# Widening a seven-product matrix product by two blocks, and moving its neighbour's partial sums into all eight PSUM banks

## The chip, the cores and the metric

One core of one Trainium2 chip runs the whole kernel. The metric is device time in microseconds (us). Three timed runs of the kernel before the change gave 512.77, 513.73 and 514.19 us; the median is 513.73 us.

## The reference

Two blocks stand one after the other. The first is a delta-rule attention over 4 batches, 8 heads, 768 positions and head size 48. The second is a three-way maxout feed-forward layer on the 3072 x 384 result.

```python
for t in range(S):                                   # attention, per batch and head
    y[t] = q[t] @ state
    v_old = k_n[t] @ state
    state += beta[t] * outer(k_n[t], v[t] - v_old)
x = y.transpose(0, 2, 1, 3).reshape(3072, 384)
h = max(max(x @ w1, x @ w2), x @ w3)                 # 384 -> 768, three times
out = h @ w_out                                      # 768 -> 384
```

All arithmetic is in 32-bit floats.

## The kernel before

**Tiling.** The sequence is cut into 12 chunks of 64 positions. Two chunks of all four batches make a group of 512 tokens, so there are six groups, m = 0 to 5. The attention of a group is done as small matrix products per head (lines with `p_g`, `p_z`, `p_j`, `p_k`, `p_q`, `p_u`, `p_s`, `p_y`) and a triangular solve on VectorE (L552, L556). The feed-forward layer of group m (`ffn(m)`) is the steady work of TensorE; the attention steps of group m+1 are laid between its pieces by hand.

**The order of the work.** The schedule is manual: each engine runs its instructions in the order in which the Python code emits them. `ffn(m)` is a generator; after each `yield` number i the main loop (L1427 to L1444) emits the attention steps that the table `LINKS` (or `LAST_LINKS` for m = 4) names for i. In that table `K0` to `K3` load four key tiles of the next group through GpSimd's queue (`load_k`, L120), and `P0`, emitted before or after them, scales a value tile on GpSimd (L287). The table names K at i = 17, so the loads of keys 4(m+2) to 4(m+2)+3 are issued while `ffn(m)` runs its output products; for m = 3 these are keys 20 to 23. Key n lies in tile `kpad[n % 4]` from n = 12 on.

**The algebra of the feed-forward layer.** From group 1 on the kernel uses max(a, b, c) = a + max(0, b - a, c - a): `less_first` replaces W2 and W3 by W2-W1 and W3-W1, and `both_layers` puts the product W1·Wo (384 x 384) into `w_sb[0][:, t, 0:384]`. The output is then h'·Wo + x·(W1Wo).

**Groups 4 and 5, the output.** `outputs(m, hs)` (L947) computes h'·Wo + x·(W1Wo) for a group. The first term goes by a seven-product scheme: the tokens are halved, the 768 hidden features are halved into two times `PAIRS` = 3 blocks of 128, and the 384 output columns are halved. Seven products replace eight; the sums of left operands (`s32`, `s14`) are made on VectorE, and the sums of right operands (t1 to t4) once in `cross_weights`. Each product is 3 blocks x 2 token tiles = 6 matmuls with 128 x 128 stationary and 128 x 192 moving operands. The second term is added plainly by four `x_times`, each 3 blocks x 2 = 6 matmuls. That makes 66 matmuls per group. Two PSUM tiles `p` and `q` take turns; ScalarE copies products out, VectorE adds.

**Group 5, the first layer.** `crossed_hidden` (L1067) does x·(W2-W1) and x·(W3-W1) by the same scheme on two of the three blocks of x; the third block is added plainly (`c1`, `c2`). It loops over six units. A unit has eight partial results, and each is one or two matmuls of 128 x 256, 11 in all. Partial results 0, 2, 3 and 4 are copied out by ScalarE (m1, m7, m5, m6); 1, 5, 6 and 7 are added by VectorE (`result`, L1108), which also does four additions between 4 and 5 and, in every second unit, four maxima (L1110). `s1` to `s4`, the sums of x's parts, are made once per group in `kmore[0]`.

**PSUM.** There are two pools of tiles, defined at L80 to L84: `ps_ffn` hands out 2 tiles of one bank each, `ps_two` hands out 3 tiles of two banks each, 8 banks together. In `crossed_hidden`, `bank(n)` takes a `ps_ffn` tile for odd n (named `p_e`) and a fresh `ps_two` tile for even n (`p_c`), of which it uses the first bank alone.

A matmul of 32-bit floats shows in the trace as two MATMUL records and two weight loads, so "x12" in a row is 6 matmuls.

Of the kernel before, what the change touches and what calls it, by code (L numbers as in the profile page):

```python
# [14 lines left out]
ALU = mybir.AluOpType  # L15
# [8 lines left out]
def kernel(  # L24
# [37 lines left out]
    KT = DM // 128  # L62
# [3 lines left out]
    GROUPS = UNITS // 4  # L66
    TOK = 512
# [12 lines left out]
    def ps_ffn(shape, name):  # L80
        return psum.tile(shape, FP32, name=name, tag="ffn", bufs=2)

    def ps_two(name):
        return psum.tile([128, 2, 512], FP32, name=name, tag="two", bufs=3)  # L84


    kpad = [const.tile([128, H, DP], FP32, name=f"kpad{i}") for i in range(4)]
# [93 lines left out]
    for bb in range(2):  # L181
        nc.gpsimd.affine_select(
            out=mask[rows(bb)], in_=mask[rows(bb)], pattern=[[1, C]], base=-1,
# [4 lines left out]
    t1 = [const.tile([128, 2, H, BL], FP32, name=f"t1{i}") for i in range(NU)]  # L188
# [5 lines left out]
    w_sb = [const.tile([128, KT, DFF], FP32, name=f"w{i}_sb") for i in range(3)]  # L194
# [112 lines left out]
    def square(name):  # L307
        return work.tile([128, H, C], FP32, name=name, tag="square", bufs=17)
# [594 lines left out]
    HALF = DM // 2  # L903
    PAIRS = FT // 2
    crossed = {}

    def cross_weights(part):

        left, right = slice(0, HALF), slice(HALF, DM)
        top, bottom = wo_sb[:, 0:PAIRS], wo_sb[:, PAIRS:FT]  # L910
        spare = w_sb[0][:, :, DM : 2 * DM]
        minus = nc.vector.tensor_tensor
        if part == 0:
            minus(
                out=spare[:, :, right], in0=bottom[:, :, right], in1=top[:, :, right],
                op=ALU.subtract,
            )
            minus(
                out=top[:, :, right], in0=top[:, :, right], in1=top[:, :, left],
                op=ALU.subtract,  # L920
            )
            return
        minus(
            out=spare[:, :, left], in0=bottom[:, :, right], in1=top[:, :, right],
            op=ALU.subtract,
        )
        fourth = []
        for n in range(2):
            t = work.tile([128, DM], FP32, name="mant", bufs=2)
            for i in range(2 - n):  # L930
                fourth.append(t[:, HALF * i : HALF * (i + 1)])
        for j in range(PAIRS):
            minus(
                out=fourth[j], in0=wo_sb[:, PAIRS + j, left], in1=spare[:, j, left],
                op=ALU.subtract,
            )
        crossed.update(
            b11=[top[:, j, left] for j in range(PAIRS)],
            b21=[bottom[:, j, left] for j in range(PAIRS)],
            b22=[bottom[:, j, right] for j in range(PAIRS)],  # L940
            t1=[top[:, j, right] for j in range(PAIRS)],
            t2=[spare[:, j, left] for j in range(PAIRS)],
            t3=[spare[:, j, right] for j in range(PAIRS)],
            t4=fourth,
        )

    def outputs(m, hs):  # L947


        xt, w = xts[m], crossed  # L950
        a11, a21, a12, a22 = (
            [hs[j + d][:, lo : lo + 256] for j in range(PAIRS)]
            for d, lo in ((0, 0), (0, 256), (PAIRS, 0), (PAIRS, 256))
        )
        p, q = (ps_ffn([128, 2, HALF], "p_o") for _ in range(2))

        def times(to, a, b, start=True, stop=True):
            for g in range(2):
                for j in range(PAIRS):
                    nc.tensor.matmul(  # L960
                        to[:, g], a[j][:, 128 * g : 128 * (g + 1)], b[j],
                        start=(start and g == j == 0),
                        stop=(stop and g == 1 and j == PAIRS - 1),
                    )

        def x_times(to, lo, right, start=False, stop=True):
            times(
                to,
                [xt[:, t, lo : lo + 256] for t in range(KT)],
                [w_sb[0][:, t, HALF * right : HALF * (right + 1)] for t in range(KT)],  # L970
                start, stop,
            )

        def held(name, dtype_bufs):
            return work.tile([128, 2, HALF], FP32, name=name, bufs=dtype_bufs)

        def store(o, cc, right, queues=one_queue):
            cols = slice(HALF * right, HALF * (right + 1))
            s0 = (2 * m + cc) * C
            for n in range(2):  # L980
                queues[n].dma_start(
                    out=out.rearrange("(b s) d -> b s d", s=S)[
                        2 * n : 2 * n + 2, s0 : s0 + C, cols
                    ].rearrange("g c x -> c g x"),
                    in_=o[rows(n)],
                )

        def op(to, a, b, how):
            nc.vector.tensor_tensor(out=to, in0=a, in1=b, op=how)

        plus, minus = ALU.add, ALU.subtract
        times(p, a11, w["b11"])
        m1 = held("m1", 1)
        nc.scalar.copy(m1, p)
        yield
        sums = [square("s").rearrange("p h c -> p (h c)") for _ in range(PAIRS)]
        s14, s32 = ([s[:, lo : lo + 256] for s in sums] for lo in (0, 256))
        for j in range(PAIRS):
            op(s32[j], a11[j], a21[j], minus)
        for j in range(PAIRS):  # L1000
            op(s14[j], a21[j], a22[j], plus)
        times(q, a12, w["b21"], True, False)
        yield
        x_times(q, 0, 0)
        c11 = held("o_sb", 2)
        op(c11, m1, q, plus)
        store(c11, 0, 0)
        yield
        times(p, s32, w["t3"])
        m7 = held("o_sb", 2)  # L1010
        nc.scalar.copy(m7, p)
        yield
        times(q, s14, w["t1"])
        m5 = held("up", 2)
        nc.scalar.copy(m5, q)
        for j in range(PAIRS):
            op(s32[j], s14[j], a11[j], minus)
        yield
        times(p, s32, w["t2"])
        m6 = held("up", 2)  # L1020
        nc.scalar.copy(m6, p)
        for j in range(PAIRS):
            op(s14[j], a12[j], s32[j], minus)
        yield
        x_times(q, 0, 1, True, False)
        op(m6, m6, m1, plus)
        op(m7, m7, m6, plus)
        yield
        times(p, a22, w["t4"], True, False)
        op(m6, m6, m5, plus)  # L1030
        op(m5, m5, m7, plus)
        yield
        x_times(p, 256, 0)
        op(m7, m7, p, plus)
        store(m7, 1, 0)
        yield
        times(q, s14, w["b22"], False)
        op(m6, m6, q, plus)
        store(m6, 0, 1)
        yield  # L1040
        x_times(p, 256, 1, True)
        op(m5, m5, p, plus)
        store(m5, 1, 1, both_queues)
        yield

    thirds = {}

    def cross_hidden(i):

# [17 lines left out]
    def crossed_hidden(m, hs):  # L1067


        xt, vec = xts[m], nc.vector.tensor_tensor  # L1070
        plus = vec if m == GROUPS - 1 else nc.gpsimd.tensor_tensor
        lo, hi = slice(0, 256), slice(256, 512)
        a11, a12, a13 = (xt[:, t, lo] for t in range(KT))
        a21, a22, a23 = (xt[:, t, hi] for t in range(KT))
        spare = [t.rearrange("p a h d -> p (a h d)") for t in kmore]
        s1, s2, s3, s4 = (spare[0][:, 256 * n : 256 * (n + 1)] for n in range(4))
# [7 lines left out]
        vec(out=s1, in0=a21, in1=a22, op=ALU.add)  # L1084
        vec(out=s2, in0=s1, in1=a11, op=ALU.subtract)
        vec(out=s4, in0=a12, in1=s2, op=ALU.subtract)
        for j in range(FT):
            hs[j] = square("h").rearrange("p h c -> p (h c)")
        for unit in range(2 * PAIRS):
            j, i = divmod(unit, 2)  # L1090
            w = {
                name: t[:, 128 * j : 128 * (j + 1)]
                for name, t in thirds[1 + i].items()
            }
# [17 lines left out]
                    )  # L1112

            def bank(n):
                return (ps_ffn([128, TOK], "p_e") if n % 2 else ps_two("p_c")[:, 0])[
                    :, 0:256
                ]

            p = bank(0)
            times(p, ("b11", a11))  # L1120
            nc.scalar.copy(m1, p)
            p = bank(1)
            times(p, ("b21", a12), ("c1", a13))
            result(top[:, lo], m1, p, c11)
            p = bank(2)
# [222 lines left out]
    def links(m, names):  # L1348
        for name in names.split():
            f, i = name[0], int(name[1])  # L1350
            if f in RECURS and m < GROUPS:
                RECURS[f](2 * m + i)
            elif f in MADE and m + 1 < GROUPS:
                MADE[f](2 * (m + 1) + i)
            elif f in UNIT and m + 1 < GROUPS:
                UNIT[f](4 * (m + 1) + i)
            elif f == "N" and m + 2 < GROUPS:
                load_blocks(4 * (m + 2) + i)
# [115 lines left out]
```

## Time and profile before

| quantity | value |
|---|---|
| timed runs, median (lowest to highest) | 513.73 us (512.77 to 514.19) |
| profiled execution, first to last instruction | 510.5 us |
| TensorE busy with matmuls | 491.1 us, 96% of the span |
| VectorE, ScalarE, GpSimd busy | 349.9, 168.7, 192.7 us |
| first-layer units of group 5 (454.1 to 484.6 us): TensorE, VectorE, ScalarE busy | 29.6, 22.8, 8.9 of 30.0 us |
| output of group 5 (484.6 us to the end): TensorE, VectorE busy | 21.7, 10.6 of 25.9 us |
| mean granted TensorE clock | 0.966 |

The profiled execution's own device time is not given apart from its span; the median of the timed runs lies 3.2 us above the span, which is work around the first and the last instruction that the profile does not show.

TensorE has work nearly all the time, but matmul records overlap and their ends are modelled, so a full busy digit can still hold short waits. The waits are read from the gaps between the starts of consecutive matmuls in the timeline.

### The profile page before, as it was taken

How to read it: one execution, taken by the hardware profiler on the slowest of the kernel's cores; microseconds unless marked ns; L12 is line 12 of the kernel's file. 1: busy time of each engine (PE TensorE's matmuls, PEld its weight loads, DVE VectorE, ACT ScalarE, POOL GpSimd, SP SyncE). 2: the span in 40 equal slices, each digit the busy share in tenths (PEclk: the TensorE clock that was granted, in tenths of full speed). 3: DMA queues.
4: the chain of work that ended last, by engine and by line, in shares of the span. 5: the costliest groups of instructions: out<-in, count | busy, mean ns of one | idle time of the engine just before them, and what ended most of it. 6: DMA issues, size and time to landing. Idle time of an engine off the chain costs nothing.

```text
span 510.5 us, 18528 instructions
## 1 busy us (share of the span) xinstructions
PE 491.1 (96%) x8016; PEld 333.1 (65%) x8016; DVE 349.9 (69%) x801; ACT 168.7 (33%) x320; POOL 192.7 (38%) x317
## 2 busy tenths in 40 slices
PE   7778989999999999999999999999999999999996
PEld 6567778756565565665555565555655556998796
DVE  5897799969996430899563987635897455456752
ACT  5585664884422242210252101252101412113210
POOL 7434372783491926670575770503130000000000
PEclk9755999999999999999999999999999999999999
DMA  8938869764055925353675454923343202230001
GB/s 111 192 64 221 194 151 155 195 199 100 5 148 140 175 46 130 99 143 83 144 136 130 120 137 94 174 37 92 80 116 81 44 3 64 54 71 2 0 17 46
DMA packets 106304, 53.49 MB, mean 105 GB/s; under 512 B 89712, under 2 KB 99984, under 8 KB 106224
## 3 DMA queue, kind: packets, MB, share of 16 engines
q1 hardware_dynamic: 94352, 31.35, 30.4%
q0 software_dynamic: 9472, 20.37, 16.4%
q8 instruction: 63, 1.03, 0.9%
q10 hardware_dynamic: 2400, 0.59, 0.6%
q14 instruction: 17, 0.14, 0.1%
HBM read 39.17 MB, written 13.11 MB: 102 GB/s over the span
## 4 chain that ended last, share of the span: by engine, by line
PE 73%; DVE 14%; DMA 5%; ACT 4%; SPq 2%; issue 2%; POOL 0%; DVEq 0%; ACTq 0%; POOLq 0%
PE p_h L1161 26%; PE p_o L1199 13%; PE p_o L960 9%; PE p_e L1102 3%; DVE tmp L552 3%; PE p_g L406 3%; PE p_c L1102 2%; PE p_m L894 2%; PE p_u L759 2%; DMA kmore<-in_k_dram 2%; PE p_k L731 2%; PE p_y L801 2%; DVE y_bl L556 2%; PE p_s L782 2%; PE p_j L714 1%
## 5 line engine op out<-in xcount | busy, mean ns | idle before, releaser
L1161 PE MATMUL p_h<-xt,w_sb 128*128 128x512 f32 (+1 forms) x450 | 187.5, 558 | 0.7 <-ACT xt L827 0.6
L1161 PEld LDWEIGHTS p_h<-xt,w_sb 128*128 128x128 f32 x450 | 82.3, 193 | 68.7 <-issue 61.8
L1199 PE MATMUL p_o<-wo_sb,h 128*128 128x384 f32 x192 | 65.3, 490 | 0.0
L1175 DVE TENSOR_TENSOR h<-h,p_h 128x512 f32<-128x512 f32 (+1 forms) x42 | 25.4, 606 | 53.9 <-PE p_h L1161 52.8
L552 DVE TENSOR_TENSOR tmp<-x_bl,y_bl 128x31 f32<-128x31 f32 (+20 forms) x139 | 51.3, 369 | 4.1
L556 DVE TENSOR_TENSOR y_bl<-y_bl,tmp 128x31 f32<-128x31 f32 (+20 forms) x139 | 48.5, 349 | 4.8
L1199 PEld LDWEIGHTS p_o<-wo_sb,h 128*128 128x128 f32 x192 | 35.7, 190 | 23.2
L364 POOL DMA_DIRECT2D turned<-in_q_dram x72 | 39.1, 551 | 4.3 <-POOL turned L359 2.9
L1205 ACT COPY o_sb<-p_o 128x384 f32<-128x384 f32 x16 | 7.7, 479 | 85.8 <-PE p_o L1199 79.8
L1171 ACT ACTIVATE h<-p_h 128x512 f32<-128x512 f32 x24 | 14.3, 597 | 63.4 <-PE p_h L1161 60.5
L254 POOL TENSOR_TENSOR w_sb<-mant,up 128x384 int32<-128x384 int32 x18 | 19.1, 1059 | 39.3 <-DVE mant L250 39.2
L406 PEld LDWEIGHTS p_g<-kqt 48*64 48x64 f32 x1216 | 24.6, 142 | 9.0 <-issue 6.4
L406 PE MATMUL p_g<-kqt 48*64 48x64 f32 (+1 forms) x1216 | 27.8, 242 | 0.9 <-ACT kqt L335 0.8
L789 DVE TENSOR_TENSOR st<-st,p_s 48x768 f32<-48x768 f32 (+1 forms) x18 | 17.1, 949 | 15.4 <-PE p_s L782 15.2
L120 POOL DMA_DIRECT2D kpad<-in_k_dram x32 | 21.8, 690 | 14.1 <-issue 12.7
L1199 PE MATMUL p_o<-w_sb,xt 128*128 128x384 f32 x72 | 25.2, 486 | 0.0
L139 POOL DMA_DIRECT2D v_t<-in_v_dram x14 | 11.5, 829 | 35.5 <-PE p_u L759 35.5
L390 DVE TENSOR_TENSOR pt<-p_g,mask 128x512 f32<-128x512 f32 x20 | 13.8, 688 | 15.9 <-PE p_g L406 15.8
L287 POOL TENSOR_TENSOR v_t<-v_t,nrm 128x768 f32<-128x768 f32 x12 | 17.9, 1493 | 9.0 <-DVE nrm L281 8.9
L359 POOL MEMSET turned<- 128x96 f32 x18 | 3.3, 192 | 47.6 <-DVE kqt L380 47.6
L759 PEld LDWEIGHTS p_u<-v_t,ut 64*64 64x64 f32 x768 | 13.4, 141 | 10.1 <-issue 7.8
L1199 PEld LDWEIGHTS p_o<-w_sb,xt 128*128 128x128 f32 x72 | 13.7, 190 | 9.5
(212 smaller groups left out, 837.0 us busy)
## 6 DMA issues: line engine op xcount, KB each, us to landing
out_dram<-o_sb SPq DMA_DIRECT2D x40, 96.0 KB
w_bits<-in_moe_w_dram SPq DMA_DIRECT2D x9, 384.0 KB
w_bits<-in_moe_w_dram POOLq DMA_DIRECT2D x9, 384.0 KB, 5.2
turned<-in_q_dram POOLq DMA_DIRECT2D x72, 48.0 KB, 2.9
kpad<-in_k_dram POOLq DMA_DIRECT2D x32, 96.0 KB, 6.1
y_x<-y SPq DMA_DIRECT2D x16, 192.0 KB
qall<-y_x SPq DMA_DIRECT2D x32, 96.0 KB
v_t<-in_v_dram POOLq DMA_DIRECT2D x14, 192.0 KB, 5.0
```

The lines of the kernel that those rows point to most:

```text
L120: queues[bb].dma_start(out=dst[rows(bb ^ g), :, 0:D], in_=src[2 * bb + g, :, c * C : (c + 1) * C, :].rearrange("h p d -> p h d"),)
L254: nc.gpsimd.tensor_tensor(out=dst.bitcast(I32), in0=mant_v.bitcast(I32), in1=up_v, op=ALU.add)
L364: (queue, nc.gpsimd)[i].dma_start(out=t[p0 : p0 + 32, bb, at : at + NP * 2 * D].rearrange("p (j x) -> p j x", j=NP), in_=(k, q)[i][2 * bb ...
L406: nc.tensor.matmul(p_g[rows(bb ^ (g * i)), par, c0 : c0 + C * (1 + whole)], kq[:, 0], kq if whole else kq[:, i],)
L552: nc.vector.tensor_tensor(out=t_v, in0=row.to_broadcast(t_v.shape), in1=column.to_broadcast(t_v.shape), op=ALU.mult,)
L556: nc.vector.tensor_tensor(out=rest, in0=rest, in1=t_v, op=ALU.subtract)
L759: nc.tensor.matmul(p_v[rows(bb ^ g), g, i], ut[c % NU][rows(bb), g, h], rhs[rows(bb), g, h],)
L960: nc.tensor.matmul(to[:, g], a[j][:, 128 * g : 128 * (g + 1)], b[j], start=(start and g == j == 0), stop=(stop and g == 1 and j == PAIRS - 1),
L1102: nc.tensor.matmul(to, w[stays], moves, start=(n == 0), stop=(n == len(terms) - 1))
L1161: nc.tensor.matmul(p_h, w_sb[i][:, t, f * 128 : (f + 1) * 128], xt[:, t, lo : lo + w], start=(t == 0), stop=(t == KT - 1),)
L1175: nc.vector.tensor_tensor(out=h, in0=h, in1=p_h, op=ALU.max)
L1199: nc.tensor.matmul(p_o, stays, moves, start=(n == 0), stop=(n == len(terms) - 1))
```

## The change

Three edits.

1. **Output of groups 4 and 5.** Blocks 0 and 1 of x·(W1Wo) become a fourth pair of blocks in the seven products: each product now has 4 blocks x 2 = 8 matmuls, and `x_times` keeps only block 2, 2 matmuls. The sums of left operands get a fourth part: for group 4 it is made beside the others on VectorE (four more 128 x 256 operations); for group 5 `s1` to `s4` of `crossed_hidden` are used again through `x_sums`. The sums of right operands are four more VectorE operations of 128 x 192 in `cross_weights(1)`, put into the tiles `kpad[2]` and `kpad[3]`.
2. **PSUM in `crossed_hidden`.** Partial results 0 to 5 now use both banks of three `ps_two` tiles: 0 and 1 share a tile, 2 and 3, and 4 and 5. Partial results 6 and 7 use the two `ps_ffn` tiles.
3. **Keys.** Keys 22 and 23 are not loaded: only the state update of the last chunk would read them, and it is left out in both kernels (`step` returns at c = 11).

```diff
@@ cross_weights(1)
+        x11, x12, x21, x22 = (w_sb[0][:, t, lr] for t in range(2) for lr in (left, right))
+        free = [kpad[i].rearrange("p h d -> p (h d)") for i in (2, 3)]
+        x1, x2, x3, x4 = (f[:, lr] for f in free for lr in (left, right))
+        for to, a, b in ((x3, x22, x12), (x1, x12, x11), (x2, x22, x1), (x4, x21, x2)):
+            minus(out=to, in0=a, in1=b, op=ALU.subtract)
...
+        for name, x in dict(
+            b11=x11, b21=x21, b22=x22, t1=x1, t2=x2, t3=x3, t4=x4
+        ).items():
+            crossed[name].append(x)
@@ outputs
+        for a, t, lo in ((a11, 0, 0), (a21, 0, 256), (a12, 1, 0), (a22, 1, 256)):
+            a.append(xt[:, t, lo : lo + 256])
...
-                for j in range(PAIRS):
+                for j in range(len(a)):
...
-                [xt[:, t, lo : lo + 256] for t in range(KT)],
-                [w_sb[0][:, t, HALF * right : HALF * (right + 1)] for t in range(KT)],
+                [xt[:, KT - 1, lo : lo + 256]],
+                [w_sb[0][:, KT - 1, HALF * right : HALF * (right + 1)]],
...
-        sums = [square("s").rearrange("p h c -> p (h c)") for _ in range(PAIRS)]
+        n = len(x_sums.get(m, ())) == 0
+        sums = [square("s").rearrange("p h c -> p (h c)") for _ in range(PAIRS + n)]
         s14, s32 = ([s[:, lo : lo + 256] for s in sums] for lo in (0, 256))
+        s1, s2, s3, s4 = s14, s32, s32, s14
+        if not n:
+            s1, s2, s3, s4 = (s + [x] for s, x in zip((s1, s2, s3, s4), x_sums[m]))
...
-        times(p, s32, w["t3"])
+        times(p, s3, w["t3"])
@@ crossed_hidden
+        x_sums[m] = s1, s2, s3, s4
+        pair = [None]
...
             def bank(n):
-                return (ps_ffn([128, TOK], "p_e") if n % 2 else ps_two("p_c")[:, 0])[
-                    :, 0:256
-                ]
+                if n > 5:
+                    return ps_ffn([128, TOK], "p_e")[:, 0:256]
+                if n % 2 == 0:
+                    pair[0] = ps_two("p_c")
+                return pair[0][:, n % 2, 0:256]
@@ links
+            if f == "K" and 4 * (m + 1) + i > 4 * GROUPS - 3:
+                continue
```

More of the change, by code (lines that the diff above doesn't have):

```diff
@@ L962, in times @@
                         start=(start and g == j == 0),
-                        stop=(stop and g == 1 and j == PAIRS - 1),
+                        stop=(stop and g == 1 and j == len(a) - 1),
                     )
@@ L995, in outputs @@
         yield
-        sums = [square("s").rearrange("p h c -> p (h c)") for _ in range(PAIRS)]
+        n = len(x_sums.get(m, ())) == 0
+        sums = [square("s").rearrange("p h c -> p (h c)") for _ in range(PAIRS + n)]
         s14, s32 = ([s[:, lo : lo + 256] for s in sums] for lo in (0, 256))
[L998 to L1001, printed above, removed]
+        s1, s2, s3, s4 = s14, s32, s32, s14
+        if not n:
+            s1, s2, s3, s4 = (s + [x] for s, x in zip((s1, s2, s3, s4), x_sums[m]))
+        for j in range(len(sums)):
+            op(s3[j], a11[j], a21[j], minus)
+        for j in range(len(sums)):
+            op(s1[j], a21[j], a22[j], plus)
         times(q, a12, w["b21"], True, False)
@@ L1012, in outputs @@
         yield
-        times(q, s14, w["t1"])
+        times(q, s1, w["t1"])
         m5 = held("up", 2)
         nc.scalar.copy(m5, q)
-        for j in range(PAIRS):
-            op(s32[j], s14[j], a11[j], minus)
+        for j in range(len(sums)):
+            op(s2[j], s1[j], a11[j], minus)
         yield
-        times(p, s32, w["t2"])
+        times(p, s2, w["t2"])
         m6 = held("up", 2)
         nc.scalar.copy(m6, p)
-        for j in range(PAIRS):
-            op(s14[j], a12[j], s32[j], minus)
+        for j in range(len(sums)):
+            op(s4[j], a12[j], s2[j], minus)
         yield
@@ L1036, in outputs @@
         yield
-        times(q, s14, w["b22"], False)
+        times(q, s4, w["b22"], False)
         op(m6, m6, q, plus)
@@ L1044, in outputs @@
         yield
-    thirds = {}
+    thirds, x_sums = {}, {}
     def cross_hidden(i):
```

## The prediction

> **What bounds the kernel now.** I read the page first, for the engine that is always busy, and its clock.
>
> ```profile
> span 510.5 us, 18528 instructions
> PE 491.1 (96%) x8016; PEld 333.1 (65%) x8016; DVE 349.9 (69%) x801; ACT 168.7 (33%) x320; POOL 192.7 (38%) x317
> PEclk9755999999999999999999999999999999999999
> PE 73%; DVE 14%; DMA 5%; ACT 4%; SPq 2%; issue 2%; POOL 0%; DVEq 0%; ACTq 0%; POOLq 0%
> ```
>
> TensorE bounds the kernel, at full clock from about 55 us on, so a matmul taken out of the tail or a wait put into it moves the end one for one. Second I read the timeline of the first-layer units of group 5 (start, duration, engine, line; "x2" is one matmul). Part of one unit, its partial results 2 to 5:
>
> ```profile
> 481.07 0.59 PE L1102 MATMUL p_e<-kmore,crossed 128*128 128x256 f32 x2
> 481.27 0.37 ACT L1127 COPY y_bl<-p_c 128x256 f32<-128x256 f32 x1 [1.11 <-PE p_c L1102]
> 481.50 0.59 PE L1102 MATMUL p_c<-kmore,crossed 128*128 128x256 f32 x2
> 481.70 0.37 ACT L1130 COPY y_bl<-p_e 128x256 f32<-128x256 f32 x1
> 481.94 0.59 PE L1102 MATMUL p_e<-xt,w_sb 128*128 128x256 f32 x2
> 482.14 0.37 ACT L1134 COPY y_bl<-p_c 128x256 f32<-128x256 f32 x1
> ```
>
> Matmuls start every 0.43 us, and a ScalarE copy of one result runs while TensorE writes the next one into another tile (481.70 beside 481.50). That overlap is what edit 2 touches. A copy starts 0.63 us after the start of the matmul it reads (481.07 to 481.70) and takes 0.37 us. Third, what a wait costs, from the seam between two units and from the seam to the output:
>
> ```profile
> 474.44 0.42 DVE L1110 SCALAR_TENSOR_TENSOR h<-h,y_bl 128x256 f32<-128x256 f32 x1
> 474.46 0.73 PEld L1102 LDWEIGHTS p_e<-xt,w_sb 128*128 128x128 f32 x4 [0.32 <-DVE y_bl L1108]
> 484.14 0.41 DVE L1108 TENSOR_TENSOR y_bl<-y_bl,p_e 128x256 f32<-128x256 f32 x1
> 484.60 3.87 PEld L960 LDWEIGHTS p_o<-wo_sb,h 128*128 128x128 f32 x24 [0.75 <-DVE y_bl L1108]
> ```
>
> TensorE restarts 0.05 us after the releasing instruction's end (484.14 + 0.41 to 484.60), and the wait holds the weight load too. The rows of the two tiles (count, then shortest, median and longest in ns) give the rest: after a wait a matmul record is 483 ns, otherwise 379, so 0.10 us is lost on weights that were not loaded ahead.
>
> ```profile
> L1102 PE MATMUL p_e<-kmore,crossed x12: 379/379/483, 455.8 to 481.3; 128*128 128x256 f32 x12
> L1102 PE MATMUL p_c<-kmore,crossed x24: 379/379/379, 455.4 to 481.7; 128*128 128x256 f32 x24
> ```
>
> Fourth, GpSimd and VectorE around the key loads:
>
> ```profile
> 371.70 2.71 POOL L120 DMA_DIRECT2D kpad<-in_k_dram  x4 [12.66 <-issue]
> 373.39 2.80 DVE L552 TENSOR_TENSOR tmp<-x_bl,y_bl 128x252 f32<-128x252 f32 x1
> 374.42 1.49 POOL L287 TENSOR_TENSOR v_t<-v_t,nrm 128x768 f32<-128x768 f32 x1
> ```
>
> An addition of 0.42 us took 2.80 beside GpSimd's scaling.
>
> **Edit 2, the banks.** Six units take 454.06 to 484.70 (the restart plus 0.10), 30.6 us, against 66 matmuls x 0.4325 = 28.5, so 2.1 us of waits are all that freer banks could give back. Partial results 0 and 1 now share a tile, as do 2 and 3, and 4 and 5. In the changed kernel's instruction stream the first matmul of results 1, 3 and 5 waits for the ScalarE copy of result 0, 2 and 4 *of the same unit*: the order is kept by tile, not by bank. In the old stream these matmuls waited for readers in earlier units. Price of one such wait: from the start of the even result's matmul to the end of its copy 0.63 + 0.37, restart 0.06, weights 0.10, less the 0.43 that it takes anyway: 0.73 us. Below, 0.57, if the weights get loaded ahead and the restart is free; above, 0.83, if the copy starts 0.73 after its matmul, as it does after a matmul that had waited (476.04 to 476.77). I take 0.73, the same copy on the same shapes behind an unhindered matmul. Three waits in six units: 18 x 0.73 = 13.1.
>
> A unit is then 4.76 + 2.19 = 6.95 us. VectorE needs at most 12 operations, four at 0.40 and four pairs at 0.79, 4.8 us a unit, so it stays under TensorE and the old 0.32 waits are gone. Six units are 41.7. Two seams come on top. In the first unit the copy of result 0 stands behind a store that ScalarE issues (454.84 for 0.68, the copy at 455.56, 1.50 after the matmul instead of 0.63): +0.87, now waited for; at least 0 if the store is out earlier. At the end the output's tile `p` takes over the buffer of result 6 instead of 5: counted from the last unit's start, copy m6 ends at 4.61, four additions to 6.26, the pair of result 5 to 7.05, the addition of result 6 at 7.46, restart 7.62 where 6.95 was free: +0.7 (before: 0.6). Sum 43.3 against 30.6: **+12.7**.
>
> On this point the Trainium skill, "PSUM — Partial Sum Buffer", section "PSUM bank collisions raise a hardware error", asks for a guard per bank and partition quadrant, and lets different banks be used at once. The rows above agree with it, a copy from one bank beside writes to another. By that rule alone the wait is not needed by the chip and edit 2 would cost nothing; the built stream has it all the same, and the stream is what runs.
>
> **Edit 1, the output.** 7 x 8 + 4 x 2 = 64 matmuls instead of 66. The 132 records of group 5 take 21.73 us on the chain, 0.33 a matmul: -0.65 a group. One cover shrinks: between the product for m6 and the next use of `p` stood an `x_times` of 6 matmuls, now of 2 (0.65 us), while the copy ends 0.68 after that `x_times` starts (496.41 to 497.09) and the restart adds 0.16: +0.2. So -0.45 for each of two groups, **-0.9**; between 0 and -1.3. VectorE's additions: 4 x 0.35 in group 4's sums lie before 434 us, needed after the p_y products at 437; the four weight sums, 4 x 0.35 = 1.4, fall into the 1.38 us that VectorE stands idle before 426.64. Beyond that cover they would hold TensorE's p_u, at most 0.3. In group 4 the last attention step p_y now follows 16 matmuls instead of 12, 1.3 us later, and with it the DMA round trip and the transpose at 449.54; TensorE's last `x_times` waits for an addition queued behind that transpose (450.69, new 452.1 to 452.7), and arrives at about 452.9. No wait, 0.2 us to spare; at most +0.5.
>
> At the end the additions to m6 and m5 are only 0.65 us apart instead of 1.95. Two stores of m6 on SP's queue took from 504.99 to about 506.2; the first store of m5 now stands behind them: **+0.6** (0 to 0.7).
>
> **Edit 3, the keys.** The four issues at 371.70 are gone, 2.71 us of GpSimd and 4 x 96 KB of transfers. Transfers beside them land earlier, y to DRAM from 371.8 among them, but the transpose that reads it (386.31) stands behind the solve on VectorE. The scaling after the issues moves up from 374.42 to right behind the four issues for keys 20 and 21 (356.31 + 2.73 = 359.04). Its collision with VectorE moves with it, into 359 to 360.8, where the subtraction L743 (359.82) is due; TensorE's p_u at 361.32 needs it and would wait 0.4. In exchange 2.4 us of VectorE return at 373, and the solve that ends at 391.7 feeds the p_z step at 400.35, which waits 0.66 for a DMA. Net **-0.2**; from -0.7 to +1.3 by those same rows.
>
> **Sum**: 12.7 - 0.9 + 0.6 - 0.2 = +12.2 us on the 510.5 span, 522.7. The median of the runs lies 3.2 above the span; carried over, 513.7 + 12.2 = 525.9 us.
>
> **Rivals.** *Faster: the pairs do not block.* If the odd results need not stand behind the copies, six units cost 28.5 + 0.8 instead of 30.6 and the rest stays: 513.7 - 1.3 - 0.5 = 511.9. It needs the wait per pair under 0.10 us (18 x 0.10 eats the 1.8); copies that begin 0.63 us after a matmul which is followed at 0.43 speak against it. *Half price.* If TensorE's queue hides the hand-over and only the 0.37 of the copy shows, 18 x 0.37 less: about 519. The recorded waits of 0.32 speak for it, but they are waits for a reader that had started long before. *The clock falls.* At 12 to 15 us TensorE was busy 1.77 of 3 us and the granted clock fell to 0.58 in the next 3; at 65 to 70 us it was busy 4.07 of 5 and kept 1.00. The new units are busy about 80% (0.47 us dead, three times in 6.95). If the clock halves throughout, 4.76 us a unit are added, up to 554; half of that, 540. The Trainium skill's "TensorE: Matmul & The Clock Gate", Part 1, gates after an idle window of some 3.4 us; by it waits of half a microsecond change nothing, and this rival adds 0.
>
> **How the numbers follow.** Full price 0.84, half price 0.06, clock 0.05, no wait 0.03, and 0.02 for a wait of up to 0.19 us, which would land within 0.3% (1.5 us, about what a measurement of this kernel can tell from no change). The first three are slower, 0.95. The likeliest case has 522.9 to 527.6 (18 x 0.57 to 18 x 0.83) and, with the smaller bounds beside it, 522.0 to 528.8; that holds 8 in 10 and is the range.
>
> **What would show it.** Right: in the units TensorE idles 0.4 to 0.5 us, released by ScalarE's copies L1142, L1148, L1155, 18 times; unit starts 6.9 us apart; 128 output records per group at 0.163; the MATMUL behind each such wait 483 ns. Wrong: units near 4.8 us, or a granted clock under 1 after 454 us; a wait at p_u near 361 over 1 us; a transpose of group 5 that holds the last `x_times` of group 4.

## The result, and the profile after

The changed kernel takes 526.45 us (median of 6 runs, 524.25 to 528.25), the kernel before, run beside it, 512.56 us (510.79 to 514.19). The ratio is 1.0262, with a 95% interval of 1.0229 to 1.0294: slower, by about 13.4 us. (The ratio, here and below, is not the quotient of the two medians; these lie 13.9 us apart.) The forecast was 525.9 us, with a range of 522.0 to 528.8. The profiled execution took 528.1 us, 1.9 us more than its span, and every timed run lies 1.7 to 1.95 us above its own span. So of the 3.2 us given ahead of the prediction for the work outside the span, some 1.3 were only that the profiled execution of before was quicker than the median.

The page of the kernel after, the lines that answer to those shown of before (span, busy time by engine, granted clock by slice, chain by engine):

```profile
span 526.2 us, 18520 instructions
PE 495.2 (94%) x8008; PEld 332.1 (63%) x8008; DVE 352.6 (67%) x809; ACT 168.8 (32%) x320; POOL 189.5 (36%) x313
PEclk9955899999999999999999999999999999999999
PE 79%; DVE 12%; ACT 3%; DMA 2%; issue 2%; SPq 1%; POOL 0%; DVEq 0%; ACTq 0%; POOLq 0%
```

TensorE issues 8 records fewer (4 matmuls) and the span is 15.7 us longer. The clock is full from about 65 us on, so what was lost is dead time of TensorE and not a slower TensorE. The timeline of the kernel after shows where: a unit of group 5's first layer, from the start of its result 0 (465.01) to the start of the next unit (471.94).

```profile
465.01 0.59 PE L1120 MATMUL p_c<-xt,w_sb 128*128 128x256 f32 x2
465.64 0.37 ACT L1142 COPY y_bl<-p_c 128x256 f32<-128x256 f32 x1 [2.95 <-PE p_c L1120]
...
466.06 1.13 PE L1120 MATMUL p_c<-xt,w_sb 128*128 128x256 f32 x4 [0.46 <-ACT y_bl L1142]
...
467.03 0.59 PE L1120 MATMUL p_c<-kmore,crossed 128*128 128x256 f32 x2
...
467.66 0.37 ACT L1148 COPY y_bl<-p_c 128x256 f32<-128x256 f32 x1 [1.65 <-PE p_c L1120]
...
468.09 1.13 PE L1120 MATMUL p_c<-kmore,crossed 128*128 128x256 f32 x4 [0.46 <-ACT y_bl L1148]
...
469.68 0.70 PE L1120 MATMUL p_c<-xt,w_sb 128*128 128x256 f32 x2 [0.46 <-ACT y_bl L1155]
...
471.94 0.59 PE L1120 MATMUL p_c<-xt,w_sb 128*128 128x256 f32 x2
```

Results 0 and 1 share one tile, results 2 and 3 the next. Result 1 (466.06) starts 0.05 us after the end of the copy of result 0 (465.64 + 0.37), 1.05 us after result 0 instead of 0.43. The same happens between 2 and 3, and, at 469.68, between 4 and 5. A unit takes 6.93 us where it took about 5. The view of waits of TensorE in the kernel after (engine, tile and line, who ended the wait; us in all, times, longest) counts them:

```profile
PE p_c L1120 <- ACT x_bl L1142: 2.2, 3, 1.3
...
PE p_c L1120 <- ACT x_bl L1155: 1.4, 3, 0.5
PE p_c L1120 <- ACT y_bl L1148: 1.4, 3, 0.5
PE p_c L1120 <- ACT x_bl L1148: 1.4, 3, 0.5
PE p_c L1120 <- ACT y_bl L1155: 1.4, 3, 0.5
PE p_c L1120 <- ACT y_bl L1142: 1.4, 3, 0.5
```

Eighteen waits in six units, all released by the three copies of even results; before there were none of these. TensorE's own row over this stretch of the kernel after (us; busy time and records of PE, PEld, DVE, ACT, POOL; granted clock; DMA share; GB/s):

```profile
457.00:500.00 43.00, 33.68 (x135) 23.62 (x133) 24.82 (x63) 8.94 (x24) 0.00 (x0) 1.00 0.06 14
```

TensorE is busy 33.68 of 43.00 us, and the granted clock is 1.00.

Cutting each profiled span at the same four instructions gives the account of the whole. The cuts are the first matmul of the p_z step at 329.8 us of before, the first output matmul of group 4, the first unit matmul of group 5, and the first output matmul of group 5. All kernels that were run are in the table, in us; the ratio to the kernel before is that of the timed runs.

| kernel | up to p_z | p_z to output 4 | output 4 | units of 5 | output 5 and end | span | from p_z on | ratio (95%) |
|---|---|---|---|---|---|---|---|---|
| before | 329.8 | 101.43 | 22.83 | 30.54 | 25.9 | 510.5 | 180.7 | 1 |
| after | 332.3 | 102.46 | 22.42 | 43.05 | 25.94 | 526.2 | 193.9 | 1.0262 (1.0229 to 1.0294) |
| e1, old banks | 334.7 | 102.54 | 22.42 | 30.57 | 25.97 | 516.2 | 181.5 | 0.9999 (0.996 to 1.0038) |
| e2, banks alone | 333.8 | 101.40 | 22.83 | 43.05 | 25.98 | 527.1 | 193.3 | 1.023 (1.0177 to 1.0283) |
| e4, spread pairs | 330.2 | 102.46 | 22.42 | 28.79 | 25.83 | 509.7 | 179.5 | 0.9988 (0.995 to 1.0025) |
| e5, one pair | 330.7 | 102.41 | 22.42 | 33.75 | 25.81 | 515.1 | 184.4 | 1.0054 (1.0023 to 1.0086) |
| e8, output alone | 331.1 | 100.85 | 22.42 | 30.55 | 25.93 | 510.9 | 179.8 | 0.9994 (0.9966 to 1.0022) |
| e6, scaling held | 329.1 | 100.86 | 22.42 | 28.76 | 25.86 | 507.0 | 177.9 | 0.9954 (0.9922 to 0.9986) |
| e7, keys and stores | 333.2 | 101.57 | 22.42 | 28.81 | 25.48 | 511.5 | 178.3 | 0.9957 (0.993 to 0.9984) |
| e9, reordered | 331.8 | 101.10 | 22.18 | 28.79 | 25.42 | 509.3 | 177.5 | 0.9944 (0.9918 to 0.997) |
| e10, both | 333.6 | 100.84 | 22.18 | 28.78 | 25.38 | 510.8 | 177.2 | 0.9938 (0.9915 to 0.9961) |

The second column, up to p_z, holds 5.6 us of spread although none of the edits acts there; the other columns repeat to 0.1 us where the code is the same, except p_z to output 4, of which more below. So the spans of single profiles can't be compared to 1 us, and the stages can. Of the 15.7 us between the two profiled spans, 2.5 were there before p_z. The rest is 1.0 in p_z to output 4, -0.4 in output 4, 12.5 in the units and about 0 at the end: 13.2 us, close to the 13.4 of the ratio.

### The profile page after: what moved, and what is told of

It is laid out like the page before. It is cut to its first block, busy times and chain, and to the rows that moved or that the text cites. A ratio compares the mean times of both kernels' runs of the same rounds, so it can differ in the third digit from the quotient of the medians.

```text
span 526.2 us, 18520 instructions
## 1 busy us (share of the span) xinstructions
PE 495.2 (94%) x8008; PEld 332.1 (63%) x8008; DVE 352.6 (67%) x809; ACT 168.8 (32%) x320; POOL 189.5 (36%) x313
## 4 chain that ended last, share of the span: by engine, by line
PE 79%; DVE 12%; ACT 3%; DMA 2%; issue 2%; SPq 1%; POOL 0%; DVEq 0%; ACTq 0%; POOLq 0%
PE p_h L1182 29%; PE p_o L1220 16%; PE p_o L972 8%; PE p_c L1120 5%; PE p_g L406 3%; DVE tmp L552 3%; PE p_u L759 2%; PE p_m L894 2%; PE p_k L731 2%; DVE y_p L556 2%; PE p_s L782 2%; PE p_y L801 2%; PE p_j L714 2%; PE p_q L731 1%; PE p_z L701 1%
## 5 line engine op out<-in xcount | busy, mean ns | idle before, releaser
L287 POOL TENSOR_TENSOR v_t<-v_t,nrm 128x768 f32<-128x768 f32 x12 | 17.9, 1491 | 9.0 <-DVE nrm L281 8.9
L1120 PE MATMUL p_c<-xt,w_sb 128*128 128x256 f32 x48 | 14.5, 405 | 6.4 <-ACT x_bl L1142 2.2
L759 PEld LDWEIGHTS p_u<-v_t,ut 64*64 64x64 f32 x768 | 13.4, 142 | 10.5 <-issue 9.7
```

The costliest lines, as they stand in the source:

```text
L287: nc.gpsimd.tensor_tensor(out=vts[c], in0=vts[c], in1=nrm[:, :, :, None].to_broadcast([128, 2, H, D]), op=ALU.mult,)
L759: nc.tensor.matmul(p_v[rows(bb ^ g), g, i], ut[c % NU][rows(bb), g, h], rhs[rows(bb), g, h],)
L1120: nc.tensor.matmul(to, w[stays], moves, start=(n == 0), stop=(n == len(terms) - 1))
```

## The experiments

All compute the whole output. Edits are shown against the changed kernel unless it says otherwise.

### e1 and e2: the banks taken back, and the banks alone

e1 is the changed kernel with the old `bank(n)`:

```diff
-                if n > 5:
-                    return ps_ffn([128, TOK], "p_e")[:, 0:256]
-                if n % 2 == 0:
-                    pair[0] = ps_two("p_c")
-                return pair[0][:, n % 2, 0:256]
+                return (ps_ffn([128, TOK], "p_e") if n % 2 else ps_two("p_c")[:, 0])[
+                    :, 0:256
+                ]
```

> The changed kernel with its old bank map (odd results in their own one-bank tiles, even ones in fresh two-bank tiles). Theory (a tile shared by neighbouring results makes TensorE wait for ScalarE's copy 18 times): six units take 30.5 us from the first matmul to the output's first, against 43.0 in the changed kernel; no TensorE wait on a ScalarE copy in the units; the total falls by 12 to 13 us below the changed kernel, within 1.5 us of the kernel before. Rival (the wider output or the missing key loads cost the time): the total stays 8 us or more above the kernel before.

e2 is the kernel before with the new `bank(n)` and nothing else of the change.

> The kernel before with the new bank map alone. Theory: units 6.93 us apart, six of them 43.0 us, the total 12 to 13 us above the kernel before (ratio about 1.024), with 18 waits of 0.46 us, the first one longer. Rival (the wider output or the keys): within 2 us of the kernel before.

e1 took 513.69 us (10 runs) against 514.26 of before: ratio 0.9999, and its units take 30.57 us, as before. e2 took 528.04 us (4 runs), ratio 1.023; with so few runs the interval is wide, 1.0177 to 1.0283, but well above 1. Its units take 43.05 us, the same to the last digit as after the whole change. The view of waits of TensorE in e2 has the same lines, with the line numbers of before:

```profile
PE p_c L1103 <- ACT x_bl L1125: 2.2, 3, 1.3
...
PE p_c L1103 <- ACT y_bl L1125: 1.4, 3, 0.5
PE p_c L1103 <- ACT x_bl L1138: 1.4, 3, 0.5
PE p_c L1103 <- ACT y_bl L1131: 1.4, 3, 0.5
```

So the 12.5 us lost in the units are edit 2 and nothing else. The two other edits together can't be told from no change in the timed runs of e1; in its stages they add 0.8 us, +1.1 before output 4 and -0.4 in it, of which more below.

### e4: all eight banks, with the partners apart

Still the two banks of three `ps_two` tiles and the two `ps_ffn` tiles, but result 3 shares the tile of 0, result 5 that of 2, and result 6 that of 4; results 1 and 7 stand alone.

```diff
-                if n > 5:
-                    return ps_ffn([128, TOK], "p_e")[:, 0:256]
-                if n % 2 == 0:
-                    pair[0] = ps_two("p_c")
-                return pair[0][:, n % 2, 0:256]
+                first = {3: 0, 5: 2, 6: 4}
+                if n in first:
+                    return pair.pop(first[n])[:, 1, 0:256]
+                if n in first.values():
+                    pair[n] = ps_two("p_c")
+                    return pair[n][:, 0, 0:256]
+                return ps_ffn([128, TOK], "p_e")[:, 0:256]
```

> The changed kernel with all eight banks in use, but results far apart sharing a tile: 0 with 3, 2 with 5, 4 with 6, and 1 and 7 alone. Theory (the wait comes from neighbours sharing a tile): by then each copy has ended (0.63 + 0.37 us after its matmul, arrival 1.7, 1.3 and 1.3 us after), so units come 4.8 to 5.0 us apart, six take 28.7 to 30 us, and the total is 13 to 14.5 us below the changed kernel and 0 to 2 us below the kernel before. Rival (use of both banks of a tile, or of all eight banks, is slow in itself because engines read beside TensorE's writes): units stay above 6 us and the total 8 us or more above the kernel before.

This is the experiment that separates the cause from its neighbours. Two things came with edit 2: more banks in use at once, and pairs in one tile. e4 keeps the first and lengthens the distance within a pair. The timeline of e4, one unit and the start of the next:

```profile
469.62 0.59 PE L1120 MATMUL p_c<-xt,w_sb 128*128 128x256 f32 x2
...
470.05 1.03 PE L1120 MATMUL p_e<-xt,w_sb 128*128 128x256 f32 x4
470.25 0.37 ACT L1144 COPY y_bl<-p_c 128x256 f32<-128x256 f32 x1 [2.22 <-PE p_c L1120]
...
470.92 1.46 PE L1120 MATMUL p_c<-kmore,crossed 128*128 128x256 f32 x6
...
474.37 0.59 PE L1120 MATMUL p_c<-xt,w_sb 128*128 128x256 f32 x2
```

A unit takes 4.75 us (469.62 to 474.37), the copy of result 0 runs beside the matmuls of result 1, and TensorE has no wait at all in the six units. They take 28.79 us: 66 matmuls at 0.4325 are 28.55, so 0.24 is left of waits, where before it was 2.0. So the number of banks in use is not what costs, and the price of edit 2 is that of placing a result beside one that is still being copied. The whole kernel comes to 512.63 us, ratio 0.9988: of the 1.75 us won in the units and 0.4 in output 4, 1.0 is lost again before output 4 (below), and what is left, 1.2, is too little for the timed runs to show.

The Trainium skill, "PSUM — Partial Sum Buffer", section "PSUM bank collisions raise a hardware error", asks that engines be kept apart by bank and quadrant, and no more. e4 agrees with it: copies from one bank run beside writes to another, at no cost. The wait of after is stricter than that rule: the trace has it released by the copy from the other bank of the same tile, so it comes from the order that this kernel keeps per tile of two banks. No run leaves that order out, so what the chip would do with an unguarded pair is not shown.

### e5: one pair left together

e4 with `first = {1: 0, 5: 2, 6: 4}`: results 0 and 1 share a tile again, 3 and 7 stand alone.

> As the spread map, but results 0 and 1 share a tile again (2 with 5, 4 with 6, 3 and 7 alone): one wait per unit instead of three. Theory: 6 waits of 0.73 us and the first one's 0.87 more (behind the store that ScalarE issues), +5.2 us over the spread map, units 5.5 us apart. If the price did not add up per wait (one wait hides others, or a fixed cost of the shared tile): +0 to 2 or +12 us.

516.64 us, ratio 1.0054. The timeline of e5, the only wait in a unit:

```profile
467.38 0.59 PE L1120 MATMUL p_c<-xt,w_sb 128*128 128x256 f32 x2
...
468.01 0.37 ACT L1144 COPY x_bl<-p_c 128x256 f32<-128x256 f32 x1 [2.22 <-PE p_c L1120]
...
468.44 1.13 PE L1120 MATMUL p_c<-xt,w_sb 128*128 128x256 f32 x4 [0.46 <-ACT x_bl L1144]
```

A unit takes 5.48 us (from 461.90 to 467.38), 0.73 more than e4's 4.75. One pair a unit costs 0.73, three cost 2.18 (6.93 less 4.75): the price per wait is the same, and it adds up without anything in common. The six units take 4.96 us more than in e4, which is 6 x 0.73, and 0.87 for the first wait, which also stands behind a store, less some 0.3 that the seam to the output gives back.

### e8 and e6: the keys

e8 is e1 with all keys loaded, so edit 1 alone. e6 is e4 with keys 22 and 23 not loaded, as in the change, but with a small write to their tiles left at the place of the loads, which GpSimd must do in its order and which waits for the last reader of the tile, as the loads did:

```diff
             if f == "K" and 4 * (m + 1) + i > 4 * GROUPS - 3:
+                if m + 1 < GROUPS:
+                    nc.gpsimd.memset(kpad[i][:, 0:1, 0:16], 0.0)
                 continue
```

> The wider output alone: keys 22 and 23 loaded again, old bank map. Prediction's step: 0.45 us saved in each of two groups, 0.6 lost at the last stores, so 0.3 us below the kernel before, a ratio of 0.999. In the trace: group 4's output 0.4 us shorter (22.4 instead of 22.8 us up to the first unit), the stretch from group 5's first output matmul to the end within 0.2 us of 25.9, and from the p_z step of group 4 to its first output matmul 101.4 us as in the kernel before (102.5 in the changed kernel). Rival: the missing key loads are not what lengthened that stretch by 1.0 us; then it stays at 102.5.

> The spread bank map, keys 22 and 23 still not loaded, but in the place of their loads two small memsets on GpSimd on parts of the same tiles, which wait for TensorE's p_s products as the loads did; so the scaling of the value tile behind them runs near 372 us again and not near 361. Theory (the scaling's collision with VectorE's solve is what costs 1.0 us, not the absence of the transfers): the stretch from p_z to the output of group 4 is back at 101.4 us or a little under, 1 us below the spread map. Rival (the transfers' absence changes something else): it stays at 102.5.

First what happened in the kernel after. Its timeline around the moved scaling (L287):

```profile
358.87 2.73 POOL L120 DMA_DIRECT2D kpad<-in_k_dram  x4
...
360.98 2.18 DVE L552 TENSOR_TENSOR tmp<-x_bl,y_bl 128x31 f32<-128x31 f32 x1
...
361.61 1.49 POOL L287 TENSOR_TENSOR v_t<-v_t,nrm 128x768 f32<-128x768 f32 x1
...
364.38 0.94 DVE L743 TENSOR_TENSOR v_t<-v_t,p_k 128x768 f32<-128x768 f32 x1
...
365.43 1.26 PE L759 MATMUL p_u<-v_t,ut 64*64 64x48 f32 x64 [1.47 <-issue]
```

The same instructions in the timeline of before:

```profile
358.42 0.18 DVE L552 TENSOR_TENSOR tmp<-x_bl,y_bl 128x31 f32<-128x31 f32 x1
...
359.82 0.95 DVE L743 TENSOR_TENSOR v_t<-v_t,p_k 128x768 f32<-128x768 f32 x1
...
361.33 1.15 PE L759 MATMUL p_u<-v_t,ut 64*64 64x48 f32 x64
```

The first addition of the solve, 31 columns wide, takes 2.18 us where it took 0.18. The five solve operations behind it and then L743, which TensorE's p_u needs, are late by that, and TensorE waits 1.5 us. (The trace names no releaser for this wait; p_u starts 0.11 us after the end of L743, and e6 below shows the connection.) From the last p_h block's start to p_u there are 4.31 us, in before 2.77. The kernels with the loads skipped and nothing in their place (after, e1, e4, e5) take 102.41 to 102.54 us from p_z to output 4.

The timeline of e6 in the same place:

```profile
357.74 0.18 DVE L552 TENSOR_TENSOR tmp<-x_bl,y_bl 128x31 f32<-128x31 f32 x1
...
359.15 0.94 DVE L743 TENSOR_TENSOR v_t<-v_t,p_k 128x768 f32<-128x768 f32 x1
...
360.65 1.15 PE L759 MATMUL p_u<-v_t,ut 64*64 64x48 f32 x64
...
369.06 0.25 POOL L1377 MEMSET kpad<- 128x16 f32 x2 [10.69 <-PE p_s L782]
369.32 1.48 POOL L287 TENSOR_TENSOR v_t<-v_t,nrm 128x768 f32<-128x768 f32 x1
```

The scaling now runs at 369.32 and meets nothing on the path: the addition is back at 0.18, p_u starts 2.77 us after its p_h block, and the stage takes 100.86. The keys are just as absent as in the changed kernel. So it is not the missing transfers that cost, but the place to which the scaling moved: 1.6 us. e6 took 511.74 us, ratio 0.9954.

With the loads in place the stage takes 100.85 (e8) to 101.57 us (e7), 101.43 in before. The difference shows in the p_z step near 400 us, the one that the prediction named: its matmuls take 2.01 us in before, with a pause for a DMA, and 1.41 in e8, almost without. From the first matmul of p_z to the next p_h block the six profiles without the loads (after, e1, e4, e5, e6, e10) all show 1.28 us; the five with them show 1.34 (e8), 1.60 (e9), 1.82 (e2), 1.94 (before) and 2.05 (e7). So leaving the loads out goes with 0.1 to 0.8 us less wait here, as the prediction expected, and the size differs from profile to profile. Whether that comes from the missing transfers or from the solve on VectorE, which is no longer held near 373 us, was not separated. Both e6 and e8 had been expected at about 101.4 and came out 0.5 shorter.

e8 took 513.59 us, ratio 0.9994: edit 1 alone can't be told from no change in the timed runs. In the stages it is worth -0.41 us in output 4 and nothing at the end.

### e7, e9, e10: towards a better version

e7 is e4 with all keys loaded, and with group 5's stores of m6 dealt to both queues, SP's and ScalarE's:

```diff
-        store(m6, 0, 1)
+        store(m6, 0, 1, both_queues if m == GROUPS - 1 else one_queue)
```

> The spread bank map with the keys loaded as before, and in group 5 the store of m6 split over SP's and ScalarE's queues. Expected: the stretch to group 4's output 1.0 us shorter than with the spread map (101.4), the stretch from group 5's first output matmul to the end 0.5 us shorter (25.3 instead of 25.8). Sum 1.5 us below the spread map, 2.5 to 3 us below the kernel before. If the end is set by the last store's own transfer and not by its place in the queue, the last stretch stays at 25.8.

510.88 us, ratio 0.9957. The stage at the end takes 25.48 us instead of 25.83 in e4: the stores that edit 1 had put behind one another cost 0.35 us, and a second queue gives it back; 0.5 had been expected.

e9 is e7 with the end of `outputs` in another order: the last seven-product matmuls for m6 come first, on `q`, so that TensorE does not go back to `p` right behind the product that ScalarE is still copying. m6 is stored early again, on one queue, and m7 last but one, on both queues. The diff is against the changed kernel, without e4's part and without the keys.

```diff
-        times(p, a22, w["t4"], True, False)
+        times(q, s4, w["b22"], False)
...
+        op(m6, m6, q, plus)
+        store(m6, 0, 1)
+        yield
+        times(p, a22, w["t4"], True, False)
...
-        store(m7, 1, 0)
+        store(m7, 1, 0, both_queues if m == GROUPS - 1 else one_queue)
...
-        times(q, s4, w["b22"], False)
-        op(m6, m6, q, plus)
-        store(m6, 0, 1)
-        yield
-        x_times(p, 256, 1, True)
-        op(m5, m5, p, plus)
+        x_times(q, 256, 1, True)
+        op(m5, m5, q, plus)
```

> As the last one, and the order of the output's products changed so that no product waits for a copy that has just begun: the product with b22 goes into q right after q's x_times, then t4 and its x_times into p, and the last x_times into q. The two waits of 0.27 us on the copy of m6 (groups 4 and 5) go, 0.4 us in all; stores of m7 and m5 in group 5 on both queues. Expected 0.4 us below the last one, 3 us below the kernel before (ratio 0.994).

510.96 us, ratio 0.9944. Output 4 falls from 22.42 to 22.18 us, which is the wait on the copy of m6's product, gone; the end falls by 0.06 only, 0.3 in all where 0.4 was expected. e10 is e9 with the keys left out and the hold of e6:

> The reordered output with the spread bank map and the split stores, and keys 22 and 23 not loaded but the scaling held back by the two memsets. Expected: the stretch from p_z to group 4's output 100.9 us (no collision near 361 us and no wait for the solve's DMA), 0.2 to 0.7 us shorter than with the keys loaded; six units 28.8; from group 5's first output matmul to the end 25.4. Total 0.2 to 0.7 us below the reordered kernel, 3 to 3.5 us below the kernel before (ratio 0.993 to 0.994).

511.27 us (12 runs) against 513.83 of before (17): ratio 0.9938. The end of e10's timeline, where two queues share the last stores:

```profile
506.36 0.60 SPq L993 DMA_DIRECT2D out_dram<-o_sb  x1
506.36 0.64 ACTq L993 DMA_DIRECT2D out_dram<-o_sb  x1
506.42 0.55 DVE L1001 TENSOR_TENSOR up<-up,p_o 128x384 f32<-128x384 f32 x1
507.04 0.85 ACTq L993 DMA_DIRECT2D out_dram<-up  x1
507.05 0.60 SPq L993 DMA_DIRECT2D out_dram<-up  x1
```

The last issue ends at 507.89, 0.92 us after the last addition (506.42 + 0.55), and the span ends at 510.8. e10 is the best version by its stages, 177.2 us from p_z on against 180.7 of before and 193.9 after; 3.5 us, or 0.7%. In the timed runs it is 0.6% faster than before, with an interval that stays below 1, and its median lies 15 us under that of after. Against e9 (177.5) the timed intervals overlap.

## Why the prediction was right, point by point

The forecast for the span was 12.2 us; the stages from p_z on show 13.2. The median came within 0.6 us of the forecast, closer than its terms deserve, since two errors met: the median of before, on which the sum was set, was 513.7 and is 512.56 in the runs beside after (1.2 less), and the two medians lie 13.9 us apart (1.7 more).

**Edit 2, price of a wait: right.** 0.73 was taken from the timeline of before; the unit of 6.95 us came out at 6.93, and e5 gives 0.73 for a single one. The copy starts 0.63 us after its matmul, takes 0.37, and the restart costs 0.05 where 0.06 was said. The 18 waits stand at the three lines named, and 18 matmul records of `p_c` take 483 ns, the others 379, as was said.

**Edit 2, the seams: right.** The first unit was to be 0.87 longer, for the store that ScalarE issues ahead of the copy. The timeline of the kernel after:

```profile
457.21 0.59 PE L1120 MATMUL p_c<-xt,w_sb 128*128 128x256 f32 x2
...
458.00 0.66 ACTq L993 DMA_DIRECT2D out_dram<-up  x1
...
458.70 0.37 ACT L1142 COPY x_bl<-p_c 128x256 f32<-128x256 f32 x1 [8.14 <-DVE kmore L1100]
...
459.13 1.13 PE L1120 MATMUL p_c<-xt,w_sb 128*128 128x256 f32 x4 [1.32 <-ACT x_bl L1142]
```

The copy begins 1.49 us after the start of its matmul, the wait is 1.32, and the first unit takes 7.80 us (457.21 to 465.01), 0.87 over the others. The seam to the output: 7.53 us from the last unit's start where 7.62 was said, 0.6 of wait where 0.7 was. Sum 43.05 against 43.3 and 12.5 us against 12.7.

**Edit 1: right in output 4, and at the end.** -0.45 was said for a group; output 4 shows -0.41. The new wait on the copy of m6's product is in the trace, +0.2 said. The timeline of after, in group 5, where the same wait stands, and the last stores:

```profile
514.22 0.48 ACT L1037 COPY up<-p_o 128x384 f32<-128x384 f32 x1 [2.12 <-PE p_o L972]
514.75 0.95 PEld L972 LDWEIGHTS p_o<-mant,h 128*128 128x128 f32 x6 [0.21 <-ACT up L1037]
...
521.49 1.94 SPq L993 DMA_DIRECT2D out_dram<-up  x3
522.14 0.64 ACTq L993 DMA_DIRECT2D out_dram<-up  x1
```

TensorE waits 0.21 for the copy, and SP's queue issues three stores without a gap, 0.65 each, the third being that of m5. At the end the forecast was -0.45 + 0.6 = +0.15; the stage shows about 0 (25.94 against 25.9). The stores' share is then some 0.5 (0 + 0.65 - 0.2), of which e7 got 0.35 back. Neither the new sums on VectorE nor the later transpose held TensorE: output 4 has no other wait.

**Edit 3: the step that failed.** "Net -0.2" was said; the stage shows +1.0, inside the stated bound of +1.3 but with the other sign. The place was right, and that the scaling would meet VectorE on the way to p_u. What failed is the wait: "TensorE's p_u at 361.32 needs it and would wait 0.4". It was 1.5, and a wait of over 1 us there was one of the prediction's own signs of being wrong. The 0.4 took VectorE as held from the start of the scaling, 359.04, to 360.8, and only the subtraction L743 as caught. The end of the block was about right: 363.16 in after, which is 360.6 when counted from the p_z step as in before (that step lies 2.5 us later in after). Its beginning was not: the operation that is held starts at 360.98, 0.6 us ahead of the scaling's record, and it is the first of the solve. Five more solve operations then stand between the end of the block and L743, which starts 2.0 us late and not 1.0. The row of 2.80 us for an addition of 0.42, shown in the prediction, begins 1.0 us ahead of its scaling too; it was read for what VectorE would regain and not for when the block begins. The gain that was to pay for it, 0.66 at p_z, was there in after's profile (1.28 us against 1.94), but its size differs from profile to profile (0.06 in e8, with all keys loaded, against the six without).

**The rivals.** *The pairs do not block*: refuted for pairs in one tile, and what it priced (28.5 + 0.8 for the units) is near what e4 gets when the partners stand apart, 28.79. *Half price*: refuted, 0.73 per wait in after, e2 and e5. *The clock falls*: refuted, 1.00 over the units at 78% busy, where the longest pause was 1.3 us. The Trainium skill, "TensorE: Matmul & The Clock Gate", Part 1, gates after an idle window of some 3.4 us, and the units agree with that. The start of before does not show such a window: there the granted clock was 0.58 from 15 to 18 us, and between the first matmul at 2.0 us and that stretch's end TensorE paused for no longer than 1.9 us (14.2 to 16.1).

## What to carry to other kernels

Where the order between engines is kept per tile, two results that follow one another must not share a tile with a reader in between, however many banks the tile has: price the pair as the time from the matmul's start to the end of the copy, plus the restart and the weight load that no longer runs ahead, less the time to the next matmul without a wait (here 0.63 + 0.37 + 0.06 + 0.10 - 0.43 = 0.73 us). Place partners so far apart that the copy has ended when the second one is due: in e4 the nearest partners start 1.3 us apart, and the copy ends 1.0 after the first. An instruction that is left out also held back what stood behind it in its queue; look where the follower lands, and whether it meets there an operation that the critical engine waits for. When an edit moves the total by less than the scatter of the start, cut the spans at fixed instructions and compare the stages.

## What the runs showed of the hardware that was not expected

**A small VectorE operation is held longer than the GpSimd record beside it.** In after an addition of 31 columns (0.18 us alone) took 2.18 us beside a scaling recorded as 1.49; in before one of 252 columns (0.42 us alone) took 2.80. Both end just behind the scaling (0.06 us in after, 0.28 in before) but begin 0.6 and 1.0 us ahead of its record, while GpSimd is still shown issuing DMAs. The Trainium skill, "SBUF — State Buffer", section "SBUF: two separate sides", calls the port pair that the two engines share an exclusive lock held for a whole instruction; the end of the held operation agrees with that, the time ahead of GpSimd's record is not in it. Why the hold begins early was only observed here: the profile's spans on GpSimd are rough, and whether GpSimd is at work on the scaling before its record begins is not shown.

**The start varies.** Up to the p_z step, where none of the edits acts, the eleven profiles differ by 5.6 us (329.1 to 334.7). The windows of 30 to 40 us (columns as in the row shown above) of before and then of after, one fence each:

```profile
30.00:40.00 10.00, 9.27 (x338) 8.60 (x338) 8.61 (x17) 7.39 (x21) 5.82 (x6) 0.50 0.33 80
```

```profile
30.00:40.00 10.00, 7.11 (x246) 6.31 (x250) 8.86 (x17) 7.74 (x19) 3.95 (x4) 0.50 0.15 24
```

At the same granted clock of 0.50 the kernel after runs 92 matmul records fewer in these 10 us, and its DMA share is 0.15 against 0.33. What sets this was not settled. The timed runs of one kernel scatter by several us too, while the later stages of the profiles repeat to 0.1 where the code is the same; that the start is the reason for that scatter as well is likely but not shown.
